# v's products in the transposes' PSUM ring, normalised unit by unit, with identity products in TensorE's early gaps and a new plan

## The chip, the core and the metric

The kernel runs on one core of a Trainium2 chip. The metric is device time in microseconds (us), from the first instruction of the program to its last, as the median of several runs. Five engines work beside each other, each in its own order: TensorE (PE: matrix products into PSUM, and transposes, which are products with an identity), VectorE (DVE), ScalarE (ACT), GpSimd (POOL) and SyncE (SP), which issues the DMAs. They meet at semaphores. [...]

## The reference

Attention with top-32 scores per row, then a dense layer with the gate h·cos(h), then a mixture of experts with a capacity. Cut to what is computed:

```python
# attention: 4 batches, 8 heads, 576 rows, 64 columns
scores = q @ k.T / 8
mask = scores >= (32nd largest score of the row)
attn = softmax(where(mask, scores, -1e9))          # sum + 1e-9 in the division
x = (attn @ v)                                     # -> 2304 tokens x 512
# dense layer, 512 -> 2048 -> 512
h = x @ w_in;  y = (h * cos(h)) @ w_out
# experts: 8, capacity 288 tokens each; greedy over the sorted logits of y @ w_gate
out[tokens of e] = relu(y[tokens of e] @ w1[e]) @ w2[e]
```

## The kernel before

**Units and blocks.** Attention runs in 72 units: a unit `j` is 128 rows of two heads that share a 128-row K tile, the first 8 units being the rows that remain over 512 (`rem`). A block is 256 tokens: eight units give one block of the dense layer, of which there are nine (blocks 0 to 8). All of attention, eight blocks' first product and seven blocks' second product run in phase 1; a tail finishes the other second products and assigns the tokens to experts; then the experts run.

**What a unit does.** `qk` (L555): the scores of 576 columns in two halves `c` of 288, each into the PSUM tile `two` (128 x 2 x 512, two banks, one head in each); `evac` (L562): ScalarE copies a half, columns 0 to 287 of both banks, into the SBUF tile `x`. There is one such PSUM buffer (`pS=1`), so a half waits for the evacuation of the one ahead. VectorE finds the 32 largest (L596 to L612), ScalarE and GpSimd mask and exponentiate (L627, L633, L640; in every second unit VectorE's L645 masks instead). `tr` (L710, in three groups `c` of three): TensorE transposes the probabilities into a buffer of the PSUM ring `pT` (two buffers of one bank each), and `eT` (L720) copies them out on ScalarE. `pv` (L735, L737; L742, L744 for `rem`): products with v. They are written into columns 288 to 415 of `two`, behind the scores, two units of a pair one in each bank (`pPV=1`).

**Normalising.** Once per pair of units (once per `rem` unit) `div` (L770, POOL) takes the row sums `rs`, `recip` (L765, DVE) inverts them, `wide` (L774, POOL) spreads them over 64 columns, `Rm` (L781, PE) transposes that into a buffer of `pT`, `Re` (L784, ACT) copies it out as `R`, and `scale` (L798, or L795 for `rem`; DVE) multiplies v's products in `two` by `R` into `xr`, the input of the dense layer.

**The dense layer.** `mm1` (L287, 12 products of 256 columns in three passes for precision) into `pH`, sine and gate on ScalarE, VectorE and GpSimd, `mm2` (L887, six products of 512 columns) into `pY`, then the logits (L923, L935).

**What sets the order.** A planner (`Plan`) makes the order of every engine. Tasks have an engine, a duration, what they come after, PSUM and SBUF buffers that they take and give, and a rank; `run` plays them with latencies between engines (`LAT`), a cost for a switch of ScalarE's table (`TABLE`) and of TensorE's tile shape (`SW`, by the shapes in `MODE`), and of the tasks that can start first takes the one of the lowest rank. `OFFSETS` (phase 1) and `TAIL_OFFSETS` (tail) are added to ranks by kind of task; `HOLD_PE` is added for a task of another tile shape. `emit` writes the tasks in that order; each engine then runs its own in this order and waits at semaphores.

Of the kernel before, what the change touches and what calls it, by code (L numbers as in the profile page):

```python
# [26 lines left out]
def f32(ap):  # L27
# [11 lines left out]
    "L": 4, "Re": 0.25, "Re_0": -5.25, "Re_r": 4.5, "Rm": 3.5, "Rm_0": -7.5, "Rm_r": -4.5, "bias": 7.25, "bias_0":  # L39
    2.75, "bias_r": -2, "big": -3, "big_0": -2.75, "big_r": -5.75, "count": -2, "div": 8, "div_0": 1.25, "div_r":  # L40
# [3 lines left out]
    -3.25, "large": 7.5, "large_0": 1, "large_r": 5.5, "less": 2.25, "less_0": 4.75, "low_in": -4.25, "low_out": 4,  # L44
# [3 lines left out]
    -5.5, "scale": -3.5, "scale_0": -1, "scale_r": -1.5, "sg_in": -10, "sg_out": 7, "shift_in": -9.75, "shift_out":  # L48
    -5.5, "sine": -4.5, "sine_0": 4, "small": 2.5, "small_0": -3.75, "small_r": -7.5, "strike": 3.75, "strike_0": 8,
    "strike_r": 6.25, "top": 7.25, "top_0": 7.25, "top_r": -3, "total": -8, "tr": -4, "tr_0": -10, "tr_r": -1.75,  # L50
    "v": 7.5, "wH_in": 6.25, "wH_out": -9.5, "wL_in": -3.25, "wL_out": -6.5, "w_in": 7, "w_out": 9.75, "whole": -5,
    "wide": -6, "wide_0": -5.25, "wl": 4, "wl_0": 3.25, "wp": 2.5, "wraw_in": 6.75, "wraw_out": -3.25, "wse": -1.75,
    "wst_out": -5.75, "wt": -9, "wte": -0.5, "xH": -5.75, "xL": -0.5, "yT": -10, "yd": -6.25, "ys": 4.75, "yt":
    0.75, "zero": 0.5, "zero_0": -5, "zero_r": -5.25
# [5 lines left out]
    "L": 3.75, "all": 0.75, "am": -3.5, "amd": -4.25, "any": -4.75, "asg": 0, "before": 0.75, "cmp": -4.75, "cnt":  # L60
    8.25, "columns": -9, "excess": -4, "first": 6.25, "gH": -6.75, "gH_e": -10, "gL": 5, "gL_e": -1.5, "gate": 1.25,
    "here": 1.75, "higher": -1.75, "hs": 1.75, "in_column": 0.5, "in_row": 1, "less": -8.5, "lg": -7, "lg4": 0.5,
    "listed": -1, "lt": 1.5, "mm1": 1.5, "mmT": 0.75, "near": -0.25, "next": -6.75, "numbers": 5.25, "places": 2.25,
    "prop": -3.75, "rise": -5.5, "rows": -3.5, "shares": 4, "sine": -3, "slots": -8, "square": -7.5, "start": 3.25,
    "sums": -5.5, "tokens": 0.25, "verdict": -2.5, "wh": 1.5, "wl": 6, "wlo": 7, "woL": 1, "woL_e": 0.75, "wrong":
    -10, "y": -1.5, "y_e": 3.25, "yd": 5, "yd_e": -0.5, "ys": -8, "ys_e": -6.75
# [3 lines left out]
class Plan:  # L70
# [6 lines left out]
    SW = 200  # L77
    HOLD_PE = 1.5
# [18 lines left out]

    def run(self):
        ts = self.tasks
        users, giver, left = {}, {}, {}  # L100
# [26 lines left out]
        while len(order) < len(ts):  # L127
# [27 lines left out]
            f = s + t["ns"] + (self.TABLE if sw else 0)  # L155
            if t["mode"]:
                f += self.SW if t["mode"] != mode else 0
                mode = t["mode"]
            free[e] = f
# [13 lines left out]
        self.end = end  # L173
        self.emit(order)

    def emit(self, order):
        for s, k in order:
            self.tasks[k]["fn"]()
# [3 lines left out]
def fused_kernel(ctx: ExitStack, tc: tile.TileContext, qT: bass.AP, kT: bass.AP, qR: bass.AP, kR: bass.AP, v9: bass.AP,  # L182
# [60 lines left out]
    def everything(fold, ctx):  # L243
# [134 lines left out]
        def phase1():  # L378
# [13 lines left out]
            for vt in vts:  # L392
# [4 lines left out]
                pS=1, pPV=1, pT=2, pH=2, pY=1,  # L397
# [87 lines left out]
            def closes(j):  # L485

                return j >= 0 and (j < NWR or (j - NWR) % 2 == 1)

# [50 lines left out]
            def qk(j):  # L539
# [27 lines left out]
                for c in range(2):  # L567
                    last = [("qk", j, 0)] if c else [("qk", j - 1, 1)] if j else []
                    add(("qk", j, c), "PE", 1160 if rem else 690, prod(c), need + last, [("pS", j, c)], give, rank=j - 1)
                    last = [("evac", j, 0)] if c else [("evac", j - 1, 1)] if j else []  # L570
                    add(("evac", j, c), "ACT", 546, evac(c), [("qk", j, c)] + last, [] if c else [("x", j)], [("pS", j, c)], rank=j - 1)

            def topk(j):
# [61 lines left out]
                def expo(h):  # L635
                    u = key(j, 0)
                    if ("rs", u) not in T:
                        new(ap, "rs", u, [128, 2, 2])
                    sums = T["rs", u][:, h, t % 2:t % 2 + 1]
# [3 lines left out]
                def zero(h):  # L643
                    sums = T["rs", key(j, 0)][:, h, t % 2:t % 2 + 1]
# [34 lines left out]
                for h in range(2):  # L679
# [5 lines left out]
                    rs = [("rs", key(j, 0))] if h == 0 and (rem or t % 2 == 0) else []  # L685
# [284 lines left out]
            if fold:  # L970
                short()
# [657 lines left out]
```

## Time and profile before

| what | us |
|---|---|
| runs | 1175.04, 1176.52, 1177.78 (median 1176.52) |
| the profiled execution | 1176.04, its span 1174.1 |
| TensorE busy | 1031.8 (88%) |
| VectorE busy | 903.1 (77%) |
| ScalarE busy | 796.9 (68%) |
| GpSimd busy | 515.2 (44%) |
| mean granted TensorE clock | 0.958 |

The profile is of one execution. Shares of busy time are means over stages of different kinds: phase 1 up to about 800 us, the tail to about 942, the experts to the end. So the stages are read one by one, and in a stage the chain of waits says which engine's work ends last. [...]

### The profile page before, as it was taken

What the parts mean: (1) busy time and instruction counts of PE and PEld (TensorE: products, weight loads), DVE (VectorE), ACT (ScalarE), POOL (GpSimd) and SP (SyncE); (2) the same over time, 40 slices, a digit from 0 to 9 for tenths busy, and PEclk for the clock granted to TensorE, in tenths of its full rate; (3) what the DMA queues carried; (4) which work ended last, traced back from release to release, by engine and by line L of the source; (5) the groups of instructions that cost most, each with busy time, mean ns of one, the idle gap of its engine ahead of it and who ended that gap; (6) DMA issues with size and microseconds to landing.
All of it is one profiled execution on the core that took longest, in us unless ns stands there. A gap on an engine that the chain in (4) does not pass through costs nothing.

```text
span 1174.1 us, 22307 instructions
## 1 busy us (share of the span) xinstructions
PE 1031.8 (88%) x7952; PEld 861.6 (73%) x7952; DVE 903.1 (77%) x2443; ACT 796.9 (68%) x1431; POOL 515.2 (44%) x645
## 2 busy tenths in 40 slices
PE   4676898999899999999999999998898599999995
PEld 1344776777677777777777777777776499999995
DVE  6989999998898888888888888886469365555530
ACT  5876798888788787787887886888341255555531
POOL 5865676666554454454454553544200202222211
PEclk9876998999999999999999999999899899999998
DMA  7564353443323323223323223210043776666611
GB/s 228 164 184 150 108 158 113 129 148 115 104 89 98 94 78 100 85 82 97 92 81 103 80 82 102 79 55 6 34 160 128 228 211 201 185 187 198 185 40 43
DMA packets 86029, 141.08 MB, mean 120 GB/s; under 512 B 15248, under 2 KB 36240, under 8 KB 85904
## 3 DMA queue, kind: packets, MB, share of 16 engines
q1 hardware_dynamic: 82832, 130.07, 36.0%
q0 software_dynamic: 3072, 9.44, 2.7%
q8 instruction: 66, 1.08, 0.4%
q14 instruction: 59, 0.48, 0.1%
HBM read 125.85 MB, written 13.63 MB: 119 GB/s over the span
## 4 chain that ended last, share of the span: by engine, by line
PE 50%; issue 16%; ACT 14%; DVE 12%; POOL 5%; DMA 2%; SPq 0%; POOLq 0%; ACTq 0%; DVEq 0%
PE pH L287 13%; PE pY L887 11%; PE two L555 7%; PE two L737 4%; PE pT L710 4%; ACT x L562 4%; DVE w L609 2%; DVE m L605 2%; POOL out L1539 2%; PE pY L1403 2%; ACT eT L720 1%; PE ph L1507 1%; PE po L1522 1%; DVE cmp L1168 1%; PE two L735 1%
## 5 line engine op out<-in xcount | busy, mean ns | idle before, releaser
L605 DVE MAX8 m<-w 128x8 f32<-128x288 f32 (+1 forms) x576 | 238.1, 449 | 0.9
L555 PE MATMUL two<-kp,qp 64*128 64x288 f32 (+1 forms) x640 | 130.2, 496 | 77.6 <-ACT x L562 62.4
L609 DVE MATCH_REPLACE8 w<-m,w 128x288 f32<-128x288 f32 x432 | 188.8, 443 | 0.0
L287 PE MATMUL pH<-xH,wiH 128*128 128x256 f32 x576 | 173.7, 302 | 1.0 <-DVE kr L318 0.6
L287 PE MATMUL pH<-xL,wiH 128*128 128x256 f32 x576 | 163.8, 284 | 0.9 <-POOL xL L853 0.9
L287 PE MATMUL pH<-xH,wiL 128*128 128x256 f32 x576 | 163.4, 284 | 0.0
L562 ACT ACTIVATE x<-two 128x576 f32<-128x576 f32 x144 | 93.1, 646 | 71.6 <-PE two L735 56.3
L555 PEld LDWEIGHTS two<-kp,qp 64*128 64x128 f32 (+1 forms) x640 | 49.8, 189 | 123.6 <-ACT x L562 89.6
L720 ACT ACTIVATE eT<-pT 128x384 f32<-128x384 f32 x224 | 106.5, 480 | 23.1 <-PE pT L710 18.0
L633 POOL TENSOR_TENSOR x<-x,w 128x576 f32<-128x576 f32 x76 | 107.3, 1424 | 20.4 <-ACT w L627 20.2
L287 PEld LDWEIGHTS pH<-xH,wiH 128*128 128x128 f32 x576 | 110.3, 191 | 7.9 <-issue 5.6
L287 PEld LDWEIGHTS pH<-xL,wiH 128*128 128x128 f32 x576 | 110.8, 192 | 1.6 <-POOL xL L853 1.3
L287 PEld LDWEIGHTS pH<-xH,wiL 128*128 128x128 f32 x576 | 110.5, 192 | 0.0
L1023 DVE TENSOR_TENSOR w2l<-w2raw,w2h 128x1024 fp32r<-128x1024 f32 x64 | 77.9, 1223 | 41.8 <-ACT w2h L1020 41.8
L710 PE MATMUL pT<-ident,x 128*128 128x128 f32 x576 | 98.3, 280 | 2.2 <-ACT wog L830 1.5
L1539 POOL DMA_INDIRECT out<-ot,idx x24 | 22.3, 928 | 177.3 <-ACT ot L1537 176.9
L887 PE MATMUL pY<-wo,gH 128*128 128x512 f32 x224 | 95.5, 426 | 0.0
L710 PEld LDWEIGHTS pT<-ident,x 128*128 128x128 f32 x576 | 68.0, 141 | 31.7 <-issue 15.5
L328 POOL TENSOR_TENSOR hs<-hs,kr 128x512 f32<-128x512 f32 x56 | 73.1, 1312 | 40.6 <-ACT kr L323 34.2
L872 POOL TENSOR_TENSOR gL<-hs,gH 128x512 fp32r<-128x512 f32 x56 | 74.7, 1334 | 35.2 <-ACT gH L868 17.7
L887 PE MATMUL pY<-wl,gH 128*128 128x512 f32 x224 | 89.1, 398 | 0.0
L887 PE MATMUL pY<-wo,gL 128*128 128x512 f32 x224 | 88.2, 394 | 0.0
(220 smaller groups left out, 2874.8 us busy)
## 6 DMA issues: line engine op xcount, KB each, us to landing
w2raw<-w SPq DMA_DIRECT2D x64, 512.0 KB, 3.7
wl<-wl_d SPq DMA_DIRECT2D x112, 256.0 KB, 2.6
vt<-v SPq DMA_DIRECT2D x48, 256.0 KB, 2.7
kp<-kT SPq DMA_DIRECT2D x32, 288.0 KB, 3.2
room<-w_in SPq DMA_DIRECT2D x16, 512.0 KB, 5.0
room<-w_out SPq DMA_DIRECT2D x16, 512.0 KB, 3.5
woL<-wl_d SPq DMA_DIRECT2D x16, 512.0 KB, 3.6
kp<-kR SPq DMA_DIRECT2D x16, 288.0 KB, 4.3
```

The costliest lines, as they stand in the source:

```text
L287: PE.matmul(ph, lw[:, c, fs], rx[:, c, :], start=(k == 0), stop=(k == 3 * KD - 1))
L328: (G if m - 1 + i in GATE_POOL else V).tensor_tensor(h, h, T["kr", m // 2][:, 2 * i:2 * i + 2], op=OP.mult)
L555: PE.matmul(o, lhsT, T["kp", us[h]][p, s], start=True, stop=True)
L562: A.activation(T["x", j][:, :, c * hS:(c + 1) * hS], T["pS", (j, c)][:, :, :hS], AF.Copy)
L605: V.max(m8_(h, 8 * k), w_(h, 0, hS + (8 if k == TOPK // 8 - 1 else 0)) if fold else w_(h))
L609: V.match_replace(w, m8_(h, 8 * k), x_(h) if k == 0 and not fold else w, -BIG)
L633: G.tensor_tensor(x_(h), x_(h), w_(h), op=OP.subtract if mode == "S" else OP.add)
L710: PE.transpose(pT[:, i, :], e[:, c0:c0 + 128], ident)
L720: A.activation(new(ap, "eT", (j, c), [128, 3, 128])[:, :n], T["pT", ("e", j, c)][:, :n], AF.Copy)
L872: (G if m in GL_POOL else V).tensor_tensor(gL, T["hs", m], f32(T["gH", m]), op=OP.subtract)
L887: PE.matmul(T["pY", blk][t], T[g, m][:, i, ts], w, start=(f == 0 and n == 0), stop=(f == KF - 1 and n == 2))
L1023: eng.tensor_tensor(WS[n][1], WR.pop(n), f32(WS[n][0]), op=OP.subtract)
```

## The change

**v's products.** `pv` takes a buffer of `pT`, 128 columns, for each unit; `two` holds scores alone. `pv` comes after the same unit's `Rm`, and the next unit's second group of transposes after `pv` (the first, in `rem` units).

**Normalising.** `div`, `recip`, `wide`, `Rm`, `Re` and `scale` run for every unit, on tiles half as wide; the tiles `rs`, `ri`, `rw` and `R` are keyed by the unit. `x_high` of a head pair waits for two `scale`s.

**Identity products.** A tile of the name `pY` is made first; where the plan's time between the end of one TensorE task and the start of the next is long, in the first 130 us of the plan, `emit` writes products of the identity with itself into it, one for each 220 ns of 65% of the gap.

**The planner.** It now follows TensorE's clock by a model of its own (`clock`), a switch of tile shape costs 95 instead of 200, `HOLD_PE` is 0 instead of 1.5, a half of `qk` is taken at 590 instead of 690 and `pv` at 985 instead of 1260. All numbers of `OFFSETS` and `TAIL_OFFSETS` are new.

```diff
 OFFSETS = {
-    "L": 4, "Re": 0.25, "Re_0": -5.25, ...
+    "L": -5.75, "Re": 1.75, "Re_0": -7.25, ...
...
-    SW = 200
-    HOLD_PE = 1.5
+    SW = 95
+    HOLD_PE = 0
...
     def emit(self, order):
+        last = 0
         for s, k in order:
-            self.tasks[k]["fn"]()
+            t = self.tasks[k]
+            if t["eng"] == "PE":
+                if self.busy and s < self.AWAKE:
+                    for _ in range(int((s - last) * 0.65 / 220)):
+                        self.busy()
+                last = self.done[k]
+            t["fn"]()
...
-                pS=1, pPV=1, pT=2, pH=2, pY=1,
+                pS=1, pT=2, pH=2, pY=1,
...
-                    add(("qk", j, c), "PE", 1160 if rem else 690, ...
+                    add(("qk", j, c), "PE", 1160 if rem else 590, ...
...
                 def prod():
-                    if rem or t % 2 == 0:
-                        T["pPV", u] = two[:, :, hS:hS + 128]
-                    o_ = T["pPV", u]
+                    o_ = new(psum, "pT", ("pv", j), [128, 128])
...
-                    if c == 0 and ("Rm", key(j - 2, 0)) in plan.tasks and closes(j - 2):
-                        last.append(("Rm", key(j - 2, 0)))
+                    if j and c == (0 if rem else 1):
+                        last.append(("pv", j - 1))
...
-                if not close:
-                    return
...
-                    G.tensor_copy(new(ap, "rw", u, [128, 2, 2, 64]), src)
+                    G.tensor_copy(new(ap, "rw", j, [128, 2, 64]), T["ri", j][:, :, None].to_broadcast([128, 2, 64]))
...
-                        V.tensor_mul(xr[:, hp].rearrange("p (t q) -> p t q", t=2), pv_, R)
+                        V.tensor_mul(xr[:, hp, t % 2 * 128:(t % 2 + 1) * 128], o_, R[:, 0])
...
+            spare = psum.tile([128, Dm], F32, name="pY")
+
+            def busy():
+                PE.matmul(spare[:, :128], ident, ident, start=True, stop=True)
+
+            plan.busy = busy
```

The change moves instructions on every engine. Three places:

TensorE in a repeating block, before: one half of a unit's scores (L555), v's products (L737, L735), one half of the next scores, transposes (L710) and the first of `mm2`'s products (L887).

```order
L555 MATMUL two<-kp,qp 128x288 x2
L737 MATMUL two<-eT,vt_121 64x128 x8
L735 MATMUL two<-eT,vt_121 64x128 x2
L555 MATMUL two<-kp,qp 128x288 x2
L710 MATMUL pT<-ident,x 128x128 x3
L887 MATMUL pY<-wo,gH 128x512
```

The same place after (L599 is `qk`, L779 and L777 are `pv`, L752 is `tr`, L812 is `Rm`, L919 is `mm2`).

```order
L599 MATMUL two<-kp,qp 128x288 x2
L779 MATMUL pT<-eT,vt_120 64x128 x8
L777 MATMUL pT<-eT,vt_120 64x128 x2
L599 MATMUL two<-kp,qp 128x288 x2
L752 MATMUL pT<-ident,x 128x128 x3
L812 MATMUL pT<-ident,rw 128x128
L919 MATMUL pY<-wo,gH 128x512
```

The row of scores, v's products, scores is the same, but v's products go into a buffer of `pT`, and of the tiles that follow in that ring of two the second (here R) takes their buffer.

VectorE in a repeating block, before: the normalisation (L798) of a pair stands behind the first look at a new unit's scores (L596); L605 and L609 are the top-32 steps, L645 masks, L765 is `recip`.

```order
L318 TENSOR_TENSOR kr<-pH,kr 128x512
L596 TENSOR_TENSOR w<-x 128x2x288
L798 TENSOR_TENSOR xr<-two,R 128x256
L645 SCALAR_TENSOR_TENSOR x,rs<-x,m_4896,w 128x576 x2
L602 TENSOR_TENSOR w<-x 128x2x288
L605 MAX m_5025<-w 128x8
L765 RECIPROCAL ri<-ri 128x4
```

After, in the same stretch (L830 is `scale`, L801 `recip`, L649, L653 and L656 the top-32 steps, L640 and L646 the looks at the scores, L688 masks).

```order
L640 TENSOR_TENSOR w<-x 128x2x288
L649 MAX m_5708<-w 128x8 x2
L830 TENSOR_TENSOR xr<-pT,R 128x128
L653 MATCH_REPLACE w<-m_5708,w 128x288 x2
L649 MAX m_5708<-w 128x8 x2
L653 MATCH_REPLACE w<-m_5708,w 128x288 x2
L649 MAX m_5708<-w 128x8
L688 SCALAR_TENSOR_TENSOR x,rs<-x,m_5590,w 128x576 x2
L649 MAX m_5708<-w 128x8
L646 TENSOR_TENSOR w<-x 128x2x288
L801 RECIPROCAL ri<-ri 128x2
```

`scale` now comes once for every unit, half as wide, among the top-32 steps.

TensorE at the start of the program, before: 28 score products in a row (seven halves), then transposes (L712, L714 are those of `rem` units).

```order
L555 MATMUL two<-kp,qp 64x288 x28
L712 MATMUL pT<-ident,x 128x128 x4
L714 MATMUL pT<-ident,x 128x128
L712 MATMUL pT<-ident,x 128x128 x4
L781 MATMUL pT<-ident,ri 128x128 x2
```

After (L1005 are the identity products).

```order
L1005 MATMUL pY<-ident 128x128 x22
L599 MATMUL two<-kp,qp 64x288 x4
L1005 MATMUL pY<-ident 128x128 x2
L599 MATMUL two<-kp,qp 64x288 x4
L1005 MATMUL pY<-ident 128x128 x12
L599 MATMUL two<-kp,qp 64x288 x4
L1005 MATMUL pY<-ident 128x128 x2
L599 MATMUL two<-kp,qp 64x288 x4
```

In all 158 identity products stand in the order ahead of the first `mm1` product, 66 of them ahead of the first transpose.

## Rows read from the trace of the kernel before

**Rows 1.** Busy time by stage: stretch, length, PE, PEld, DVE, ACT, POOL, PEclk, DMA share, GB/s

```profile
0.00:127.00 127.00, 80.43 (x610) 47.14 (x611) 108.00 (x317) 85.11 (x166) 85.65 (x94) 0.81 0.58 177
127.00:283.00 156.00, 139.87 (x1081) 113.57 (x1079) 146.06 (x394) 134.67 (x254) 104.89 (x114) 0.96 0.40 127
...
452.50:539.00 86.50, 79.81 (x618) 64.83 (x618) 74.83 (x225) 68.81 (x123) 42.20 (x56) 1.00 0.30 89
```

**Rows 2.** Chain that ended last, whole run: start us, us, what

```profile
452.54 1.50 PE pY L887 x6
...
539.00 1.50 PE pY L887 x6
```

**Rows 3.** The same chain within one block, 452 to 539 us

```profile
460.23 0.69 PE two L555 x4
460.92 1.02 PE two L737 x16
461.94 0.27 PE two L735 x4
462.24 0.66 ACT x L562
462.94 0.76 PE two L555 x4
463.69 0.48 PE pT L710 x3
...
465.82 0.33 PE pT L710 x3
...
522.16 1.28 ACT L640
...
532.39 0.44 PE pT L923 x4
```

**Rows 4.** Waits 452.5 to 539 us: who waited for whom, us in total, times, longest

```profile
PE two L555 <- ACT x L562: 6.2, 8, 0.8
...
DVE w L596 <- ACT x L562: 4.5, 2, 4.0
DVE xr L798 <- PE two L555: 4.1, 2, 3.4
DVE kr L318 <- ACT kr L308: 1.9, 1, 1.9
DVE w L596 <- POOL x L633: 0.9, 1, 0.9
...
ACT x L562 <- PE two L735: 8.1, 7, 2.2
```

**Rows 5.** Groups by shape: shapes, count, busy us, mean ns, idle before and releasers

```profile
L720 ACT ACTIVATE eT<-pT 128x128 f32<-128x128 f32 x8 | 2.2, 279 | 0.0
L784 ACT ACTIVATE R<-pT 128x256 f32<-128x256 f32 x40 | 15.3, 383 | 2.2 <-PE pT L781 2.0
L798 DVE TENSOR_TENSOR xr<-two,R 128x256 f32<-128x256 f32 x32 | 13.4, 420 | 26.5 <-PE two L555 25.9 <-ACT R L784 0.3
L774 POOL COPY rw<-ri 128x256 f32<-128x256 f32 x32 | 13.4, 420 | 11.4 <-DVE ri L765 11.4
L765 DVE RECIPROCAL ri<-ri 128x4 f32<-128x4 f32 x32 | 5.2, 161 | 0.3 <-POOL ri L770 0.3
L795 DVE TENSOR_TENSOR xr<-two,R 64x128 f32<-64x128 f32 x16 | 4.6, 288 | 4.5 <-PE two L555 4.1
```

**Rows 6.** Busy time of the first 127 us in two stretches, columns as in rows 1

```profile
0.00:30.00 30.00, 14.22 (x50) 4.33 (x52) 20.06 (x63) 15.23 (x24) 16.07 (x20) 1.00 0.72 229
30.00:127.00 97.00, 66.21 (x562) 42.81 (x559) 87.94 (x255) 69.88 (x143) 69.58 (x75) 0.75 0.54 161
```

**Rows 7.** VectorE's waits, 30 to 127 us, columns as in rows 4

```profile
DVE xr L795 <- PE two L555: 4.1, 2, 2.4
DVE w L596 <- ACT x L562: 2.6, 2, 2.3
```

More of the change, by code (lines that the diff above doesn't have):

```diff
@@ L50 @@
[L50 to L54, printed above, removed]
+    "L": -5.75, "Re": 1.75, "Re_0": -7.25, "Re_r": 6.5, "Rm": 3.75, "Rm_0": 1.5, "Rm_r": 7.25, "bias": 7.75,
@@ new lines @@
+    "recip": 1.75, "recip_0": -0.5, "recip_r": 3.5, "scale": -7, "scale_0": -6.75, "scale_r": -6.25, "sg_in": 0,
+    "sg_out": -0.25, "shift_in": 2.75, "shift_out": -6.25, "sine": 5.25, "sine_0": -9.75, "small": 1.5, "small_0":
+    5, "small_r": 4.25, "strike": 2.75, "strike_0": 10, "strike_r": 7, "top": -2.5, "top_0": 5, "top_r": 5.25,
+    "total": 7, "tr": -0.25, "tr_0": 1.75, "tr_r": -1, "v": 5.25, "wH_in": -5, "wH_out": -6.5, "wL_in": -6.75,
+    "wL_out": -2.25, "w_in": 7.75, "w_out": 10, "whole": -1.75, "wide": 5.5, "wide_0": -2.5, "wl": -1.25, "wl_0":
@@ L59 @@
 TAIL_OFFSETS = {
[L60 to L66, printed above, removed]
+    "L": 5.25, "all": -6.25, "am": -7.5, "amd": 5, "any": -0.5, "asg": 6.75, "before": -5, "cmp": -8, "cnt": -1.75,
+    "columns": 2.75, "excess": -5.75, "first": 1.5, "gH": 1.5, "gH_e": 1, "gL": 5, "gL_e": 0.5, "gate": -3.5,
+    "here": 1.5, "higher": 2.25, "hs": -3.25, "in_column": -1.75, "in_row": 4, "less": 3.25, "lg": -4.75, "lg4":
+    -1.5, "listed": -7, "lt": -1.25, "mm1": -2.25, "mmT": 4.25, "near": 5, "next": 2.5, "numbers": 7.75, "places":
+    2, "prop": -7, "rise": -0.75, "rows": 6.25, "shares": -0.75, "sine": 0.25, "slots": -6, "square": -1.5, "start":
+    -5.5, "sums": 6, "tokens": -0.5, "verdict": 3.5, "wh": -7, "wl": -7.75, "wlo": -4.75, "woL": -8.5, "woL_e": -6,
+    "wrong": -7, "y": 0.75, "y_e": 1.75, "yd": 3.75, "yd_e": 1.25, "ys": 0.75, "ys_e": 4.75
 }
@@ L96, in add, with clock, work, roll @@
                                mode=self.MODE.get(kind, "128x128") if eng == "PE" else None)
+    IDLE, FULL, WINDOW = 0.38, 0.8, 3413
+    AWAKE = 130000
+    busy = None
+    def clock(self):
+        act, slow, since, W = 0.0, False, 0, self.WINDOW
+        def work(s, w):
+            nonlocal act, slow, since
+            def roll(t):
+                nonlocal act, slow, since
+                while t >= since + W:
+                    a = act / W
+                    if not slow and a < self.IDLE and since > self.AWAKE:
+                        slow = True
+                    elif slow and a >= self.FULL:
+                        slow = False
+                    act, since = 0.0, since + W
+            roll(s)
+            t = s
+            while w > 1e-9:
+                speed = 0.5 if slow else 1.0
+                can = (since + W - t) * speed
+                if w <= can:
+                    act += w / speed
+                    t += w / speed
+                    w = 0
+                else:
+                    act += since + W - t
+                    w -= can
+                    t = since + W
+                    roll(t)
+            return t
+        return work
     def run(self):
         ts = self.tasks
+        work = self.clock()
         users, giver, left = {}, {}, {}
@@ L808, in pv @@
-                firstw = j == 0 if rem else (j - NWR) % (2 * HP) == 1
-                add(("scale", j), "DVE", 620 if rem else 345, scale, [("Re", u), ("pv", j)], [("xr", blk)] if firstw else [],
-                    [("R", u), ("pPV", u)], rank=rank)
+                        V.tensor_mul(xr[:, hp, t % 2 * 128:(t % 2 + 1) * 128], o_, R[:, 0])
+                exps = [("zero" if MODES[j] == "T" else "exp", a) for a in range(2 * j, 2 * j + 2)]
+                add(("div", j), "POOL", 190, div, exps, [("ri", j)], [("rs", j)], rank=rank)
@@ new lines, in pv @@
+                add(("recip", j), "DVE", 85, recip, [("div", j)], rank=rank)
+                if not rem:
+                    add(("wide", j), "POOL", 300, wide, [("recip", j)], [("rw", j)], [("ri", j)], rank=rank)
+                add(("Rm", j), "PE", 220 if rem else 110, spread, [("recip" if rem else "wide", j)], [("pT", "R", j)],
+                    [("ri" if rem else "rw", j)], rank=rank)
+                add(("Re", j), "ACT", 265 if rem else 165, spread_out, [("Rm", j)], [("R", j)], [("pT", "R", j)], rank=rank)
```

80 lines of the change are left out of this document (36 added, 44 removed), and 9 rows, old and new, of the table OFFSETS.

## The prediction

> **What bounds the kernel now.** I read the stages first, then the chain of waits inside one stage, then the waits of single engines.
>
> The stages [rows 1]: in the first 127 us VectorE is busy 108.0 of 127 and TensorE 80.4, at a mean granted clock of 0.81. From 127 to 283 us VectorE is busy 146.1 of 156. Then comes a stretch in which blocks repeat, 283 to 791 us: the same six pY products stand at 452.54 and at 539.00 us [rows 2], so a block (eight units of attention) lasts 86.46 us and the stretch holds 508 / 86.46 = 5.88 of them. In one such block TensorE is busy 79.81 us, VectorE 74.83 and ScalarE 68.81, at full clock [rows 1]. After 856 us come the routing and the experts.
>
> Inside a block the chain of waits [rows 3] runs almost wholly on TensorE, and it leaves TensorE always at the same spot: half of a score product (0.69 us from 460.23), v's products (1.02 + 0.27), and then, before the next half of a score product, an evacuation of `two` on ScalarE (462.24, 0.66 us) during which TensorE stands still. ScalarE's own waits say why: it stands idle 7 times in the block, 8.1 us, until v's products are done before it evacuates [rows 4]. It doesn't read them: the scores lie in columns 0 to 287 of `two`, v's products behind them, in the same two banks. TensorE waits 6.2 us in the block for that evacuation, in 8 pieces of 0.78 [rows 4], and 79.8 + 6.2 is all but 0.5 of it. So TensorE sets the pace there, and nearly all that it loses is this wait. VectorE has the same thing in mirror image: 4.1 us in the block in which its normalisation (`scale`, which reads `two`) waits for the score product [rows 4].
>
> [...]
>
> **The change part by part.** The sum is made against the profiled execution, 1176.04 us (span 1174.1 and 1.94 around it); the median of the runs shown is 1176.52, 0.5 above it.
>
> *v's products leave `two`.* Each unit's products now get a buffer of the ring `pT`, alone in its bank. TensorE's order around the spot stays as it is in most units (score half, v's products, score half), so the evacuation can start when the first half ends and has v's 1.29 us to run its 0.66 in [rows 3]. That takes 6.2 us per block off TensorE, if ScalarE is free then. In one spot of eight it isn't: at 522.16 a table load (1.28 us) stands in ScalarE's chain ahead of the evacuation [rows 3]. I leave one wait of 0.8 us per block.
>
> *The ring is fuller.* Its two buffers served 3.5 tiles a unit (three groups of transposes and half a tile R) and now serve five. v's tile is held until `scale` on VectorE has read it. In about five units of eight the next user of that buffer follows after a score half (0.69) and three transposes (0.33 to 0.48), 1.0 to 1.2 us later. What has to fit in: the way over (0.03), `scale` (about 0.3 [rows 5]) and the way back (0.04, both ways as between TensorE and ScalarE now [rows 3]), 0.4 us, plus the instruction that VectorE is just in. No row shows this wait. Its lower bound is 0, its upper bound per place one VectorE wait of the kind seen now, 4.0 us [rows 4]. I take 0.35 us at five places, 1.7 per block, since VectorE has only some 12 us of slack per block and the two engines now meet once per unit; the nearest row is the present wait of 0.78, and I take under half of it because 0.6 us or more of slack stands ahead.
>
> *Normalising per unit instead of per pair.* 32 more each of `div`, `recip`, `wide`, `R`'s evacuation and `scale`, at half width; the transposes that spread R stay 80. VectorE: `recip` 32 x 0.16 = 5.2 us; `scale` was 32 x 0.420 = 13.4 and is 64 x (0.288 to 0.420), taken at 0.29 (128 elements, as in the narrow form) = 18.6 [rows 5]. Together +10.4 us over 64 units, 1.3 per block: VectorE 76.1 per block. ScalarE: 64 x 0.279 - 32 x 0.383 = +5.6 us, 0.7 per block [rows 5]. GpSimd, at 42.2 of 86.5 busy [rows 1], gains at most 64 x 0.42 = 26.9 us [rows 5], 3.4 per block. All three stay below TensorE's 79.8, so I cost them at nothing on the path; VectorE's cover is 82.6 - 76.1 = 6.5 us and it is the first that would run out (below).
>
> *The new order.* Offsets, the price of a switch of TensorE's tile shape (200 to 95) and the reluctance to switch (1.5 to 0) change, so the whole plan does. Switches of shape go from 305 to 355, but in the repeating blocks from 32 to 33 or 34 (38 in one). Entering the full array from a score product costs 0.48 - 0.33 = 0.15 us [rows 3]; two per block are 0.3. Where the streams stand to each other hardly changes: 17 units are through their top-32 at the second block's first product in both orders, 66 at the eighth's.
>
> So a block after: 79.8 + 0.8 + 1.7 + 0.3 = 82.6 us, a gain of 3.9, and 5.88 x 3.9 = 22.7 us. Bounds: 79.8 + 0.3 = 80.1 (37 us gained) and, with the ring at the present price of 0.78 in all eight units, 87.1 (4 us lost).
>
> *127 to 283 us.* The same block with the output weights' conversion beside it; VectorE is idle 9.9 of 156 [rows 1], and no gain can pass that. I take 4.
>
> *Identity products at the start.* 158 products of 128 x 128 in places where the plan sees TensorE idle in the first 130 us. No row shows this product. Transposes of that size go at 0.11 (four in 0.44), ten of v's products, two by two in one array, at 0.26 a pair [rows 3]. So 17 to 41 us at full clock; I take 0.26, since they are plain products. TensorE is idle 46.6 of the first 127 us, so they fit, and at full clock the real work shrinks too: 66.2 us busy at 0.75 in 30 to 127 us is about 50 at 1.0 [rows 6]. What this can give is bounded by VectorE, which sets the pace there: idle 9.1 us from 30 to 127, of which 4.1 wait for a score product beside v's products and 2.6 for an evacuation [rows 6, 7]. I take 4, with -5 to +9 as bounds.
>
> From 0 to 30 us the granted clock is 1.00 although TensorE is busy only 14.2 of 30 us [rows 6], so the products placed there keep up nothing that had fallen. [...]
>
> *The rest.* The tail's offsets change too (791 to 942 us), with no part of it named by the diff: 0, with 6 us either way. The experts keep their code: 0.
>
> Sum: 1176.04 - 22.7 - 4 - 4 = 1145.3; with the median's 0.5, **1146 us**.
>
> **The rivals.**
> (a) *ScalarE or VectorE is next.* 29 loads of exp's table over 72 units are 3.2 per block. If each holds up an evacuation by its 1.28 us [rows 3], 4.1 us of waits stay: 79.8 + 0.3 + 1.7 + 4.1 = 85.9 per block, 0.6 x 5.88 = 3 us gained there and 8 before, 1165 us. VectorE's 76.1 and its waits that remain (4.5 + 1.9 + 0.9 [rows 4]) give 83.4, 1150 us. For it: ScalarE will be busy 69.5 us in a block. Against it: in seven of eight spots it stood idle before the evacuation [rows 4]. Time 1158 to 1173.
> (b) *Slower by the ring.* VectorE stands up to 4.0 us at one wait for scores, 4.5 per block in 2 pieces [rows 4]. If `scale` is queued behind such a wait, v's tile keeps its buffer, the transposes stop TensorE for 4.0 + 0.4 - 1.1 = 3.3 us, twice per block, 6.6. A block is 82.6 + 6.6 = 89.2: 2.7 x 5.88 = 16 us more, less 8 of the start: 1184 us. It decides as soon as stalls in the ring pass 6.2 - 0.8 - 0.3 = 5.1 us per block, 0.64 per unit. Against it: `scale` now stands in VectorE's order amid the top-32 instructions of another unit, not behind an evacuation.
> (c) *The products arrive late.* If the clock falls in spite of them each takes 0.52 us, 82 in all; with 80 of real work that is 162 us where there are 127, so the start is 35 us later: 1146 + 35 = 1181. Against it: the clock of 1.00 up to 30 us.
> (d) *It doesn't do what it says*: another dependence (the x buffer that the evacuation overwrites, which the transposes of three units earlier read) holds the evacuation as v's products do now. Then nothing moves: 1176.
>
> **How the numbers follow.** Forecast (1124 to 1158) 0.58; (a) 0.20; (d) 0.05; (b) 0.12; (c) 0.04; below 1124 0.01. About 0.2% (2.4 us) is what a measurement of this kernel can tell from no change: faster 0.79, within it 0.05, slower 0.16. The range leaves out the slower cases and the far end below: 1124 to 1176.
>
> **What would show it.** Right: blocks of 81 to 84 us at full clock, TensorE's waits for the evacuation of `two` down from 6.2 to about 1 us per block, ScalarE's wait for v's products gone from its list, and a new wait of `pT`'s transposes for `scale` of under 3 us per block; a granted clock above 0.9 from 30 to 127 us, with the first pH product only some 4 us earlier. Wrong: blocks of 86 us and more with TensorE's wait moved to `scale` (b) or still on the evacuation behind a table load (a), or a first pH product later than 127 us (c).

## The result, and the profile after

The changed kernel takes **1122.18 us** (median of 4 runs, 1120.81 to 1124.64); the kernel before, on the same chip, 1176.24 (1175.04 to 1177.78). The ratio is 0.9542, interval 0.9522 to 0.9562: 54 us faster. The forecast was 1146, 31 us faster, with a range of 1124 to 1176. The direction and the mechanism were right, the size was not.

The profiled execution has a span of 1120.1 us, of which TensorE is busy 1050.0 (94%), VectorE 913.2 (82%), ScalarE 794.0 (71%) and GpSimd 533.3 (48%).

I cut both kernels at the same events: the first pH product after the start, the end of the first block (block 0, its first `ys` evacuation), the end of the seventh (block 6, its second and last `ys` evacuation), the first product for the gate's logits (`pp`), and the first of the experts' products. Start of each event, us:

| | first pH | block 0 done | block 6 done | `pp` | experts | profiled span |
|---|---|---|---|---|---|---|
| before | 118.9 | 282.8 | 790.6 | 826.5 | 936.8 | 1174.1 |
| after | 123.1 | 276.1 | 749.3 | 780.0 | 882.9 | 1120.1 |

Between the second and third column lie six blocks: 84.63 us each before, 78.87 after. (From first evacuation to first evacuation they are 84.33 and 78.67: the columns also hold the 1 to 2 us between block 6's two evacuations.) So of the 54 us, 6.7 came up to the first block's end, 34.6 in the six blocks, 5.2 from there to `pp`, 7.4 from `pp` to the experts, and nothing behind. The last two have to be read together, since the new tail does work ahead of `pp` that stood behind it (e3, below). Busy time by stage, first of after and then of before (columns as in [rows 1]); the rows that start at 282.80 and 276.10 are the six blocks, those behind them lead up to `pp`:

```profile
123.00:276.10 153.10, 140.14 (x1082) 114.60 (x1080) 145.84 (x407) 130.10 (x253) 108.41 (x127) 0.98 0.39 128
276.10:749.30 473.20, 472.71 (x3675) 384.23 (x3675) 452.36 (x1394) 412.62 (x758) 270.07 (x384) 1.00 0.32 96
749.30:780.00 30.70, 27.44 (x259) 25.24 (x256) 22.62 (x73) 24.64 (x50) 15.69 (x31) 1.00 0.15 53
```

```profile
282.80:790.60 507.80, 468.44 (x3606) 378.95 (x3603) 442.76 (x1325) 405.82 (x725) 249.27 (x332) 1.00 0.30 89
790.60:826.50 35.90, 27.20 (x258) 24.59 (x257) 26.00 (x83) 27.83 (x52) 17.76 (x31) 0.93 0.11 42
```

TensorE is busy 472.71 of 473.20 us: for six blocks it all but never stops. Before, it stood 39.4 of 507.8. The waits of the same stretch say the same (who waited for whom, us in total, times, longest; after, then before):

```profile
PE pT L812 <- DVE xr L830: 0.4, 1, 0.4
...
DVE xr L830 <- PE pT L777: 8.1, 19, 1.5
...
ACT x L606 <- PE two L599: 4.2, 8, 1.0
...
ACT x L606 <- PE pT L752: 3.3, 6, 1.0
```

```profile
PE two L555 <- ACT x L562: 37.2, 48, 0.8
...
DVE xr L798 <- PE two L555: 22.8, 12, 3.4
...
ACT x L562 <- PE two L735: 46.3, 42, 2.2
```

TensorE's wait for the evacuation of `two`, 37.2 us in 48 pieces, has gone altogether; so has ScalarE's wait for v's products, 46.3 us in 42 pieces. What is left of ScalarE's waits before the evacuation is for the score product itself (4.2 us) and for the transposes that read the x buffer (3.3). The whole of TensorE's new wait in the ring `pT` is one of 0.4 us. It is the other way round: `scale` on VectorE waits for v's products, 8.1 us in 19 pieces.

The chain that ended last, in the spot of [rows 3] that answers to 460.23 to 463.69 (start us, us, what):

```profile
477.05 0.69 PE two L599 x4
477.73 1.02 PE pT L779 x16
478.76 0.22 PE pT L777 x4
478.97 0.69 PE two L599 x4
479.66 0.48 PE pT L752 x3
480.14 0.11 PE pT L812
```

Score half, v's products, score half, with nothing between them. How much one old stop cost is read best from start to start. TensorE's timeline of after at such a spot, and that of before (start us, us, instruction, [idle before it <- releaser]):

```profile
466.24 0.39 PE L777 MATMUL pT<-eT,vt 128*64 128x128 f32 x4
466.56 0.76 PE L599 MATMUL two<-kp,qp 64*128 64x288 f32 x4
```

```profile
461.77 0.39 PE L735 MATMUL two<-eT,vt 128*64 128x128 f32 x4
462.94 0.76 PE L555 MATMUL two<-kp,qp 64*128 64x288 f32 x4 [0.78 <-ACT x L562]
```

The score half starts 0.32 us after the start of the last group of v's products now, and started 1.17 after it: 0.85 for an idle time of 0.78, since the two groups overlap by 0.07 in the trace and a stop takes that overlap too. This is one spot, and the ends of TensorE's products in the trace are modelled.

The normalisation by unit, over the whole run (shapes, count, busy us, mean ns, idle before):

```profile
L830 DVE TENSOR_TENSOR xr<-pT,R 128x128 f32<-128x128 f32 x64 | 18.3, 286 | 20.9 <-PE pT L777 18.7 <-ACT kr L371 1.7
L807 POOL COPY rw<-ri 128x128 f32<-128x128 f32 x64 | 23.7, 371 | 19.8 <-DVE ri L801 13.7 <-PE pT L812 3.4 <-PE two L599 1.0
...
L816 ACT ACTIVATE R<-pT 128x128 f32<-128x128 f32 x64 | 17.5, 274 | 2.5 <-PE pT L812 2.5
```

`scale` at 0.286 us and R's evacuation at 0.274 are what was taken for them (0.29 and 0.279, from the narrow forms of [rows 5]); GpSimd's copy, at 0.371, is inside its bound of 0.42.

### The profile page after: what moved, and what is told of

Same layout as the page of the kernel before. It is cut to its first block, busy times and chain, and to the rows that moved or that the text cites. A ratio compares the mean times of both kernels' runs of the same rounds, so it can differ in the third digit from the quotient of the medians.

```text
span 1120.1 us, 23056 instructions
## 1 busy us (share of the span) xinstructions
PE 1050.0 (94%) x8268; PEld 890.8 (80%) x8268; DVE 913.2 (82%) x2507; ACT 794.0 (71%) x1461; POOL 533.3 (48%) x709
## 4 chain that ended last, share of the span: by engine, by line
PE 57%; issue 16%; DVE 14%; POOL 5%; ACT 5%; DMA 2%; SPq 0%; POOLq 0%; ACTq 0%; DVEq 0%
PE pH L335 16%; PE pY L919 13%; PE two L599 7%; PE pT L752 5%; PE pT L779 5%; DVE m L649 2%; DVE w L653 2%; PE pY L1441 2%; POOL out L1577 2%; PE ph L1545 1%; PE po L1560 1%; DVE cmp L1206 1%; DVE room L487 1%; PE pT L777 1%; DVE w L646 1%
## 5 line engine op out<-in xcount | busy, mean ns | idle before, releaser
L649 DVE MAX8 m<-w 128x8 f32<-128x288 f32 (+1 forms) x576 | 237.5, 449 | 1.5
L653 DVE MATCH_REPLACE8 w<-m,w 128x288 f32<-128x288 f32 x432 | 188.2, 442 | 0.0
L599 PE MATMUL two<-kp,qp 64*128 64x288 f32 (+1 forms) x640 | 118.5, 455 | 7.5 <-ACT x L606 6.4
L762 ACT ACTIVATE eT<-pT 128x384 f32<-128x384 f32 x224 | 104.0, 477 | 28.4 <-PE pT L752 24.6
L677 POOL TENSOR_TENSOR x<-x,w 128x576 f32<-128x576 f32 x76 | 109.7, 1460 | 20.1 <-ACT w L671 20.0
L752 PE MATMUL pT<-ident,x 128*128 128x128 f32 x576 | 98.3, 283 | 2.2 <-ACT eT L762 1.9
L919 PE MATMUL pY<-wo,gH 128*128 128x512 f32 x224 | 96.1, 429 | 0.0
L752 PEld LDWEIGHTS pT<-ident,x 128*128 128x128 f32 x576 | 67.6, 143 | 29.2 <-issue 14.9
L919 PE MATMUL pY<-wl,gH 128*128 128x512 f32 x224 | 88.6, 396 | 0.0
L919 PE MATMUL pY<-wo,gL 128*128 128x512 f32 x224 | 87.9, 393 | 0.4 <-POOL gL L904 0.4
L1058 ACT ACTIVATE w2h<-w2raw 128x1024 fp32r<-128x1024 f32 x64 | 67.0, 1052 | 23.7 <-DMA w2raw<-w 23.7
```

The costliest lines, as they stand in the source:

```text
L599: PE.matmul(o, lhsT, T["kp", us[h]][p, s], start=True, stop=True)
L649: V.max(m8_(h, 8 * k), w_(h, 0, hS + (8 if k == TOPK // 8 - 1 else 0)) if fold else w_(h))
L653: V.match_replace(w, m8_(h, 8 * k), x_(h) if k == 0 and not fold else w, -BIG)
L677: G.tensor_tensor(x_(h), x_(h), w_(h), op=OP.subtract if mode == "S" else OP.add)
L752: PE.transpose(pT[:, i, :], e[:, c0:c0 + 128], ident)
L762: A.activation(new(ap, "eT", (j, c), [128, 3, 128])[:, :n], T["pT", ("e", j, c)][:, :n], AF.Copy)
```

## The experiments

What had to be told apart: whether the gain is the bank (v's products in `two` make TensorE wait for ScalarE, as the prediction had it) or the planner's numbers (offsets, prices, durations), which put everything in another order; what the identity products and the tail's offsets give; and what would bound the kernel next, VectorE's load or the hold of the ring. Each edit is against the changed kernel unless it says otherwise. Start of the events in the runs, us:

| | first pH | block 0 done | block 6 done | per block | `pp` | experts |
|---|---|---|---|---|---|---|
| e2_back_in_two | 124.4 | 286.1 | 794.4 | 84.72 | 823.7 | 922.9 |
| e4_old_numbers | 125.8 | 282.4 | 777.4 | 82.50 | 814.1 | 913.9 |
| e5_new_numbers | 127.1 | 282.4 | 773.7 | 81.88 | 809.8 | 915.3 |
| e9_old_offsets | 117.0 | 292.7 | 750.2 | 76.25 | 809.4 | 909.8 |
| e3_old_tail | 122.5 | 277.4 | 750.5 | 78.85 | 781.4 | 890.7 |
| e1_no_products | 123.7 | 278.6 | 751.8 | 78.87 | 782.5 | 881.2 |
| e6_late_products | 124.1 | 278.3 | 751.4 | 78.85 | 782.1 | 883.4 |
| e10_no_products_again | 123.3 | 278.3 | 751.5 | 78.87 | 782.2 | 882.2 |
| e11_changed_again | 123.4 | 276.3 | 749.5 | 78.87 | 780.1 | 879.3 |
| e7_scale_twice | 122.0 | 275.4 | 755.3 | 79.98 | 786.3 | 887.8 |
| e8_idle_product | 123.5 | 282.0 | 768.2 | 81.03 | 799.2 | 900.4 |

### The bank by itself: e2_back_in_two

v's products go into `two` again, unit by unit, in the plan and order of the changed kernel (the reading for the remainder units follows).

```diff
-                    o_ = new(psum, "pT", ("pv", j), [128, 128])
-                    if rem:
-                        o_ = o_.rearrange("p (h q) -> p h q", h=2)
+                    o_ = T["pT", ("pv", j)] = two[:, :, hS:hS + 64] if rem else two[:, t % 2, hS:hS + 128]
```

> The changed kernel in the same order, with v's products written again behind the scores in `two` instead of into a buffer of `pT`. Theory A (the shared bank is the cause): TensorE's wait for the evacuation returns, 0.7 to 0.8 us per unit, blocks of 84 to 86 us instead of 78.9, time 1155 to 1170 us. Theory B (the new order and its numbers are the cause): blocks stay below 81 us, time below 1135.

Measured: 1165.77 us (1162.36 to 1170.06), ratio to before 0.9913 (0.9890 to 0.9937). Blocks are at 84.72 again, and in this order v's products in `two` cost 1165.77 - 1122.18 = 43.6 us. Its waits, 285 to 770 us:

```profile
ACT x L606 <- PE two L775: 37.8, 35, 1.9
...
PE two L599 <- ACT x L606: 22.8, 30, 0.8
DVE xr L828 <- PE two L599: 19.8, 16, 2.2
```

The three old waits are back where only the place of v's products was put back: that this place causes them is shown by itself. One thing is left open: v's products left the tile `two` and its banks at the same time, so no run here tells a shared bank from a shared tile. TensorE's wait makes 22.8 / 485 x 84.72 = 4.0 us of the block's 5.85; a part of the rest may be the 0.07 us that a stop cost beside its idle time at the one spot above: by an estimate 30 x 0.07 = 2.1 us of the 485, 0.4 per block.

### The numbers: e4_old_numbers, e5_new_numbers, e9_old_offsets

e5 is the kernel before, tail included, with phase 1 planned by the new numbers; e4 is the new structure and the new tail, with phase 1 planned by the old ones; e9 is as e4, with the old offsets alone. None has identity products. The new numbers include the planner's model of TensorE's clock, which e5 and e9 have and e4 hasn't. What e5 changes in the kernel before, beside `OFFSETS` (e4 sets all of it back, e9 only `OFFSETS`):

```diff
-    SW = 200
-    HOLD_PE = 1.5
+    SW = 95
+    HOLD_PE = 0
...
-                    add(("qk", j, c), "PE", 1160 if rem else 690, prod(c),
+                    add(("qk", j, c), "PE", 1160 if rem else 590, prod(c),
...
-                add(("pv", j), "PE", 1700 if rem else 1260, prod,
+                add(("pv", j), "PE", 1700 if rem else 985, prod,
```

> v's products in the ring and normalising per unit, but phase 1 planned with the old offsets, switch price 200, reluctance 1.5 and old durations of scores and v's products; no identity products; the tail as in the changed kernel. Theory A (the bank is the cause and a plan only has to be fair): blocks of 79 to 83 us, time 1125 to 1150. Theory B (the numbers fitted to the new structure are the cause): blocks of 84 us and more, time 1155 to 1185.

> The kernel before (v's products behind the scores, normalising per pair, old tail), with phase 1 planned with the new offsets, switch price 95, reluctance 0 and new durations; no identity products. Theory A (the bank is the cause): TensorE still waits about 6 us per block for the evacuation, blocks of 84 to 90 us, time 1165 to 1200. Theory B (the numbers are the cause): blocks below 82 us, time below 1145.

> The new structure with the planner's new durations, switch price and reluctance, but phase 1's old offsets; no identity products; new tail. Theory A (the planner's truer durations do most of what the numbers do): blocks of 79 to 80.5 us, time 1122 to 1135. Theory B (the offsets, fitted to the new structure, do it): blocks of 81.5 us and more, time 1140 to 1160, as with all old numbers (1154.6).

Measured: e4 1154.56 us (1154.20 to 1155.68), ratio 0.9815 (0.9791 to 0.9838); e5 1156.28 (1154.68 to 1157.16), 0.9828 (0.9804 to 0.9853); e9 1149.59 (1148.46 to 1152.99), 0.9791 (0.9769 to 0.9814). Either half alone gives some 20 us, both together 54. The new tail, which e4 has and e5 hasn't, is worth 8.5 us in the changed kernel (e3, below). If it is worth as much in e4, the structure without it gives 1176.2 - 1163.1 = 13 us, the numbers 20, and both (e3) 45.5: 12 us more than the two added. So neither theory holds alone: v's place in `two` is the lock, and the order has to use the room that opens without it.

Where the halves differ stands in the six blocks. e4, busy time and waits:

```profile
282.40:777.40 495.00, 476.92 (x3636) 380.72 (x3634) 459.49 (x1377) 405.71 (x751) 280.50 (x380) 1.00 0.31 91
```

```profile
PE two L600 <- ACT x L607: 8.8, 12, 1.3
...
PE pT L753 <- DVE xr L831: 3.3, 4, 0.8
```

Here TensorE still stands 18.1 us of 495, 3.0 per block: it waits 8.8 us for evacuations that ScalarE gets to late, though v's products no longer hold them, and 3.3 in the ring for `scale`; smaller waits in the ring make most of the rest. In e5, with v's products in `two`, the order by itself halves the pieces of the old wait, 24 where there were 48:

```profile
PE two L603 <- ACT x L610: 15.1, 24, 0.8
```

e9 shows what offsets do beside durations and prices. Its busy time by stage, and that of e1 (all numbers new, no products):

```profile
123.00:292.70 169.70, 149.61 (x1144) 119.94 (x1144) 161.74 (x440) 142.82 (x277) 117.23 (x138) 0.96 0.39 122
292.70:750.20 457.50, 456.70 (x3485) 369.88 (x3483) 421.96 (x1275) 386.02 (x705) 257.38 (x356) 1.00 0.33 98
750.20:809.40 59.20, 48.51 (x382) 39.92 (x380) 47.19 (x152) 46.22 (x88) 25.90 (x48) 0.86 0.09 33
```

```profile
123.00:278.60 155.60, 142.93 (x1083) 117.36 (x1081) 145.19 (x404) 130.44 (x253) 108.79 (x127) 0.96 0.39 125
```

With the new durations TensorE is unbroken in the blocks of e9 too (456.70 of 457.50), but the streams stand otherwise to each other: the first block is done 14.1 us later than in e1, with 16.6 us more of VectorE's work ahead of it, and from block 6 to `pp` it takes 59.2 us where e1 takes 30.7; TensorE stands 10.7 of them, at a clock of 0.86. The block mean of 76.25 is therefore no gain: work has only moved out of that stretch. The time is what theory B forecast, the blocks are what neither did. Durations, prices and the clock model together give 1154.56 - 1149.59 = 5 us, or 3 by the ratios, whose intervals overlap; the offsets on top of them give 28 (1149.59 to the 1121.55 of e10). Which of the offsets do it was not tried.

### The tail: e3_old_tail

`TAIL_OFFSETS` of before, and the tail planned with the old prices:

```diff
+        plan.SW, plan.HOLD_PE, plan.AWAKE = 200, 1.5, 1e18
```

> The changed kernel with the tail planned by the old tail offsets, switch price and reluctance. Theory A (the 7.3 us between the first gate product and the experts, 116.0 before and 108.7 now, are the tail's own new order): 115 to 117 us again, time 1128 to 1130. Theory B (they come from a state in which phase 1 now leaves the engines): 108 to 110 us, time 1121 to 1124.

Measured: 1130.68 us (1129.38 to 1135.11), ratio 0.9622 (0.9575 to 0.9669): the tail's order is worth 8.5 us. In the profiles 6.6 of them lie between block 6's end and the experts (140.2 us in e3, 133.6 after; 146.2 before), and one wait stands out. TensorE's waits there, before and then e3; and the chain over the same place, before, e3 and after:

```profile
PE pp L355 <- DVE wog__9620 L1077: 8.4, 1, 8.4
```

```profile
PE pp L403 <- DVE wog__10171 L1115: 7.6, 1, 7.6
```

```profile
826.50 3.64 PE pp L355 x32
```

```profile
781.37 3.64 PE pp L403 x32
```

```profile
773.23 6.08 PE pH L335 x48
...
779.99 1.93 PE pp L403 x32
```

With the old tail the first thing that TensorE has to do after phase 1 is `pp`, and it stands for 8 us until VectorE has copied the gate's weights. The copy takes 0.56 us (e3), but it stands in VectorE's order behind the last work of phase 1 and the preparation of the tail's constants, and starts only at 780.45. Now 48 pH products stand ahead of `pp` and cover that time. So the wait lay ahead of `pp`, and the 48 products behind it: the gain shows behind `pp` (109.3 us to the experts in e3, 102.9 after, 110.3 before), while the stretch from block 6 to `pp` is as long in e3 as after, 30.9 and 30.7 us, with TensorE busy 21.4 of it in e3 and 27.4 after. The stretch in e3:

```profile
750.50:781.40 30.90, 21.41 (x215) 19.41 (x211) 22.43 (x72) 22.55 (x45) 15.91 (x31) 0.92 0.15 52
```

The granted clock falls with the stop too: in e3 TensorE stands from 773.8 to 781.4 us, the granted clock is 0.50 from 776.5 to 786.7, and the same 32 `pp` products take 3.64 us behind the stop and 1.93 behind the pH products.

### The identity products: e1_no_products, e6_late_products, e10_no_products_again, e11_changed_again

e1 (and e10, the same kernel) leaves all of them out, e6 those that the plan places in the first 25 us (52 of 158). e11 is the changed kernel again, beside e10.

```diff
-            plan.busy = busy
```

```diff
-                if self.busy and s < self.AWAKE:
+                if self.busy and 25000 <= s < self.AWAKE:
```

> The changed kernel with the 158 identity products left out and the same order otherwise. Theory A (they hold the granted clock up while VectorE sets the pace, and are worth a few us): granted clock from 30 to 127 us back near 0.75 to 0.85, first pH product 3 to 8 us later than 123.1 us, time 1125 to 1131 us against 1122. Theory B (VectorE hides TensorE's clock there): clock down as well, but time within 2 us of 1122.

> The changed kernel with the identity products of the first 25 us of the plan left out (52 of 158), the later ones kept. Theory A (the row of the kernel before: the clock is at 1.00 up to 30 us without them): same clock later, time within 2 us of 1122. [...]

> The changed kernel without the identity products once more, beside the changed kernel itself, to bound what the products are worth. Theory A (VectorE hides TensorE's clock at the start): within 2.5 us of the changed kernel. Theory B (the clock is worth something): 3 us slower or more.

> The changed kernel itself, as the other side of that comparison. Both theories: 1120 to 1125 us.

Measured: e1 1125.14 us (1121.18 to 1127.79), e6 1122.01 (1119.73 to 1124.01); then, side by side, e10 1121.55 (1120.92 to 1124.20) and e11 1120.78 (1118.49 to 1123.54), ratios 0.9543 (0.9527 to 0.9558) and 0.9534 (0.9516 to 0.9552). The 3 us of e1 did not come again: all the products together are worth 0.8 us, which these runs can't tell from nothing. The profiles show a little more: with all the products `pp` starts at 780.0 and 780.1 us (after, e11), without them at 782.5 and 782.2 (e1, e10), and without the earliest at 782.1 (e6). But from `pp` to the experts the same tail took 98.7 to 102.9 us in these five profiles, so that 2 us do not stand out in the time. The products do to the clock what they are for. The first 127 us, without them and with them:

```profile
0.00:30.00 30.00, 14.79 (x54) 4.43 (x56) 20.14 (x62) 15.90 (x25) 16.14 (x20) 1.00 0.72 222
30.00:127.00 97.00, 66.28 (x561) 42.89 (x560) 95.06 (x264) 71.11 (x148) 69.72 (x79) 0.79 0.56 166
```

```profile
0.00:30.00 30.00, 25.79 (x178) 20.43 (x178) 19.76 (x56) 14.56 (x23) 13.16 (x19) 1.00 0.75 232
30.00:127.00 97.00, 78.93 (x759) 58.76 (x759) 95.37 (x266) 73.16 (x151) 71.75 (x80) 0.93 0.53 163
```

From 30 to 127 us the clock rises from 0.79 to 0.93, and VectorE stays at 95 of 97 us. It sets the pace there: the first pH product comes at 123.1 and 123.4 us with the products, at 123.7 and 123.3 without.

### What is next: e7_scale_twice, e8_idle_product

e7 writes each whole unit's `scale` twice: VectorE gets more work, and v's tile is held longer in the ring. e8 adds a product of the same size between SBUF tiles behind `scale`, which holds nothing in the ring.

```diff
                         V.tensor_mul(xr[:, hp, t % 2 * 128:(t % 2 + 1) * 128], o_, R[:, 0])
+                        V.tensor_mul(xr[:, hp, t % 2 * 128:(t % 2 + 1) * 128], o_, R[:, 0])
```

```diff
+            idle = mp.tile([128, 128], F32, name="idle")
...
+                        V.tensor_mul(idle, xr[:, hp, t % 2 * 128:(t % 2 + 1) * 128], R[:, 0])
```

> The changed kernel with `scale` of the 64 whole units written twice, so v's buffer of the ring is held about 0.3 us longer and VectorE has 2.3 us more per block (75.4 to 77.7 of 78.9). Theory A (the ring's hold is covered by 1 us of other products, VectorE has the reserve): blocks below 80 us, time up by 0 to 6 us. Theory B (the prediction's step: the two engines meet in the ring at every unit and pay for it): TensorE waits for `scale` 1.5 us per block and more, time up by 10 us or more, and clearly more than in the next run.

> The changed kernel with one product of the same shape more on VectorE after each `scale`, on SBUF tiles into a tile that nobody reads, so VectorE's load is as in the run with `scale` twice but the ring's buffer is not held. Theory A: the same as there within 3 us. Theory B: at least 5 us faster than there. If both are 15 us and more above 1122, VectorE's load is the next bound and not the ring.

Measured: e7 1128.04 us (1127.19 to 1129.99), 0.9606 (0.9590 to 0.9623); e8 1140.30 (1138.83 to 1141.76), 0.9707 (0.9689 to 0.9725). The added instruction and TensorE's waits for `scale` (285 to 745 us), first of e7, then of e8:

```profile
L831 DVE TENSOR_TENSOR xr<-pT,R 128x128 f32<-128x128 f32 x64 | 18.7, 291 | 2.2
```

```profile
PE pT L752 <- DVE xr L831: 1.4, 1, 1.4
PE pT L812 <- DVE xr L831: 0.7, 1, 0.7
```

```profile
L832 DVE TENSOR_TENSOR idle<-xr,R 128x128 f32<-128x128 f32 x64 | 26.9, 421 | 2.2
```

```profile
PE pT L813 <- DVE xr L831: 3.9, 4, 2.1
```

e7 came out as theory A has it, e8 as neither. The two were meant to differ in the hold of the ring alone, but e8's product took 0.421 us in the mean where e7's took 0.291, so its load was larger too. The mean hides two kinds (least, median and longest in ns):

```profile
L832 DVE TENSOR_TENSOR idle<-xr,R x64: 291/293/1271, 138.1 to 792.1; 128x128 f32<-128x128 f32 x64
```

```profile
426.23 1.27 POOL L906 TENSOR_TENSOR gL<-hs,gH 128x512 fp32r<-128x512 f32 x1
426.56 1.09 DVE L832 TENSOR_TENSOR idle<-xr,R 128x128 f32<-128x128 f32 x1
```

43 of the 64 take 0.29 to 0.30 us, like e7's; the other 21 take 0.33 to 1.27 and end 0.14 to 0.15 us after a GpSimd instruction that had begun before them, as here (427.50, 427.65). `scale`, with one operand in PSUM, never takes more than 0.293 us in e8. So in 21 places e8's product lasts until a GpSimd instruction has ended, and the pair doesn't separate the hold from the load as planned. What e7 shows alone is that doubling the hold costs 6 us for 18.7 us of work, with 2.1 us of TensorE's waits in the ring for it: VectorE has some reserve left, and the ring's hold is not what binds. e8 lost 18 us for 26.9 of added work without that hold. How much of it is VectorE's other work getting longer (its masked product over 576 columns went from 0.844 to 0.953 us) was not separated.

No run was clearly faster than the changed kernel: e11 (the same kernel), e10 and e6 lie within 1.4 us of it.

## Why the prediction was right and wrong, point by point

**What bounds the kernel, and the bank: right.** The wait of [rows 4] that was named has gone, together with ScalarE's and VectorE's halves of it, and e2 brings all three back (22.8, 37.8 and 19.8 us). In e2 ScalarE waits 37.8 us for products whose columns it doesn't read; why it has to is not shown, since no run tells the shared bank from the shared tile.

**The block, 82.6 us: the step that failed.** It was 78.87. Three terms were added to TensorE's busy time: 0.8 for one late evacuation, 1.7 for stalls in the ring, 0.3 for switches of shape. The first came out at 0; of the second one wait of 0.4 us in six blocks, 0.07 per block. TensorE's idle time fell from 39.4 us to 0.5, or by 6.5 per block. Its busy time is 472.71 / 6 = 78.8 us per block, 0.7 above the 78.07 of before, so that the shape of the sum was right and 5.8 per block came out, where it had 3.9. The base of 79.8 came from one block of 86.46 us [rows 1, 2] where the mean of six is 84.63. That is not what failed: with the means the same terms give 78.07 + 2.8 = 80.9, 3.8 less per block and 22.6 us in all. What failed is that the two waits were kept, 2.5 us per block, and they rest on the sentence "Where the streams stand to each other hardly changes". With the new structure and the old numbers (e4) such leftovers are there: TensorE stands 3.0 us per block, for late evacuations (8.8 us in all) and in the ring (3.3 for `scale`). That e4's block of 82.50 is the forecast one is in part luck, since its busy time of 79.5 per block is above the mean of before. I had priced the new structure in the old order; the new order takes the leftovers away. In it VectorE is first at the ring (it waits 8.1 us there for TensorE in 19 pieces; in e4 3.5 in 4), and the engine that sets the pace waits there for 0.4 us. In time: 34.6 - 22.7 = 11.9 us more than the sum had.

**The tail, 0 with 6 either way: the second step that failed.** It gave 12.6 us from block 6's end to the experts, by two ways. 6.0 came with phase 1's new numbers and structure: e3, with the old tail, takes 140.2 us for it and the kernel before 146.2. TensorE has 5.8 us less to do there up to `pp` (busy 21.4 us, 27.2 before), and 4.3 more in the six blocks ahead: work has moved forward. The other 6.6 (140.2 to 133.6) came with the tail's own order, which covers the wait for `wog_` and the granted clock of 0.50 that goes with it. That wait, 8.4 us in one piece, stood in the trace of before; the prediction named no wait of that stage, though new offsets for it could move one, and so put 0. These two steps make up the error: 11.9 + 12.6, less 1.3 of the next point, is 23 of 24.

**Up to the first block's end, 8 us: nearly right, for half a wrong reason.** It was 6.7. But the first pH product was forecast 4 us earlier and comes 4.2 later, and e1 without products ends its first block at 278.6, so that some 4 of the 6.7 us are order and v's new place and not the products. That VectorE bounds what the products can give was right. They take 0.30 us each, 48 us for 158 (two entries of the trace for each), where 0.26 and 41 were taken:

```profile
L1005 PE MATMUL pY<-ident 128*128 128x128 f32 x316 | 47.9, 300 | 1.4 <-POOL ident masks.py:199 1.4
```

**The clock of the first 30 us: wrong.** The row of [rows 6] says 1.00, and I took it that nothing had fallen. What TensorE did there says otherwise. Its timeline without the products (e1), and with them (after):

```profile
10.33 2.19 PE L599 MATMUL two<-kp,qp 64*64 64x288 f32 x8 [0.75 <-ACT x L606]
```

```profile
1.36 7.82 PE L1005 MATMUL pY<-ident 128*128 128x128 f32 x44 [1.36 <-POOL ident masks.py:199]
9.10 1.19 PE L599 MATMUL two<-kp,qp 64*64 64x288 f32 x8
```

Eight entries of score products, all of one shape, take 2.19 us in e1, where TensorE was busy 2.45 of the first 10 us, and 1.19 behind 7.8 us of identity products, although the clock's column says 1.00 for the first 30 us of both. The trace of before has such groups of eight entries early, and at both values of the granted clock that its records have, 0.50 and 1.00 (timeline, then the busy time of the two stretches):

```profile
10.44 2.18 PE L555 MATMUL two<-kp,qp 64*64 64x288 f32 x8 [0.75 <-ACT x L562]
...
38.44 2.18 PE L555 MATMUL two<-kp,qp 64*64 64x288 f32 x8 [1.88 <-ACT x L562]
...
45.07 1.19 PE L555 MATMUL two<-kp,qp 64*64 64x288 f32 x8
```

```profile
36.80:43.60 6.80, 5.16 (x51) 3.47 (x51) 6.42 (x16) 4.95 (x11) 6.16 (x8) 0.50 0.39 121
43.70:57.20 13.50, 8.50 (x87) 4.93 (x85) 13.38 (x43) 11.64 (x24) 10.87 (x12) 1.00 0.72 234
```

So the score products of the first 30 us went as slowly as at a granted clock of 0.50; in e1 eight of their entries still take 2.18 us at 25.60. The traces show why the column says otherwise: their records of the clock begin at 33.4 us in the kernel before, 33.5 in e1 and 6.9 after, each with one at 1.00, and the view gives 1.00 where there is no record. So [rows 6] held no measurement of those 30 us, and the forecast should have gone by these durations, which stood in the trace of before. Going by the row cost the sum little: e6, without the earliest products, takes the same time by the runs (1122.01), though its `pp` starts 2.1 us later than after's.

**VectorE, ScalarE and GpSimd at nothing on the path: right**, and narrowly so for VectorE. It went from 442.76 to 452.36 us in six blocks, 1.6 per block where 1.3 was forecast, and is now busy 95.6% of the stretch; e7 and e8 show that a further 19 to 27 us of work on it are paid in part, 6 and 18 us.

**The rivals.** (a) did not come, but it is what e4 shows in part, so it was a real one that the order removed. (b) and (c) did not come: 0.4 us in the ring, and a first pH product at 123.1 us with the products and 123.7 without. The 0.52 us of (c), twice 0.26, stands in no row that the prediction names: the groups of eight entries above took 2.18 us at a granted clock of 0.50 and 1.19 at 1.00, 1.83 times as long, and of after's identity products the 24 entries that start from 1.4 to 6.4 us took 0.421 us in the median, the 118 from 6.6 to 35.3 us 0.275. (d) shows as 3.3 us of ScalarE's waits for the transposes, which TensorE doesn't feel.

## What to carry to other kernels

Where an engine that sets the pace waits for another at one spot, removing the cause and reordering around it are one change: here each alone gave 13 to 20 us and both together 45; in e4's and e5's traces the waits that the one leaves behind are those that the other removes. If a change replaces an order, price every single long wait of the pacing engine in every stage that is reordered. Filling TensorE's gaps to hold its clock (0.93 from 30 to 127 us, 0.79 without) bought 0.8 us by the runs and some 2 by the profiles, where another engine was busy 95 of 97 us.

## What the runs showed of the hardware

- The granted clock that the profile shows was 1.00 in the first 30 us of a run in which score products took 2.19 us that take 1.19 behind earlier work. The trace of that run (e1) has no record of the clock before 33.5 us, and the view gives 1.00 where there is none: there the durations showed the speed, and that column did not.
- Eight entries of score products, of one shape, took 2.18 us at a granted clock of 0.50 (at 38.44 us of before) and 1.19 at 1.00 (at 45.07).
- A stop of TensorE cost more than its idle time at the spot that was read: 0.85 us from start to start for 0.78 of idle, by ends of products that are modelled.
- A stop of 7.6 us (e3) was followed by slower products: 32 `pp` products took 3.64 us at a granted clock of 0.50, and 1.93 where 48 products stand ahead of them.
- A VectorE product of 128 x 128 elements took 0.29 us, with one operand in PSUM (at most 0.293) as with both in SBUF (43 of 64). The other 21 of those with both in SBUF took up to 1.27 us, and each ended 0.14 to 0.15 us after a GpSimd instruction that had begun before it (e8).
